# Attention and an ELU feed-forward block on one core: in the first chunk, three float32r terms for the first product of nine tiles, plain float32 for every second product

## The chip, the core and the metric

The kernel runs on one core of a Trainium2 chip. The metric is the device time of one execution in microseconds (us), the median of several runs. TensorE (PE in the profile) multiplies matrices, VectorE (DVE) and ScalarE (ACT) do elementwise work, GpSimd (POOL) a little of it, and SyncE (SP) issues the DMAs. Each engine takes its instructions strictly in the order in which the program lists them.

## The reference

```python
scores = q @ k.transpose(0, 1, 3, 2) / sqrt(D)      # 8 batches, 8 heads, 576 positions, D = 64
# heads 0-3: the last 32 positions; heads 4-7: every fourth of the last 128
attn = softmax(where(mask, scores, -1e9))
x = (attn @ v).transpose(0, 2, 1, 3).reshape(4608, 512)
h = x @ w_in                                        # w_in 512 x 2048
g = where(h > 0, h, exp(minimum(h, 0)) - 1)         # ELU
out = g @ w_out                                     # w_out 2048 x 512
```

The weights reach the kernel in float64's 64 bits (as int64), and it makes float32 of them on the chip.

## The kernel before

The 4608 rows of `x` are done in nine chunks `c` of 512, and the 2048 hidden columns in sixteen tiles `f` of 128. For each tile, `gemm1(c, f)` computes the first product into a PSUM bank (`h_ps`, two of them in turn), `elu` makes the hidden tile of it on ACT and DVE, and `gemm2`, two tiles later (`LAG`), adds that tile times its rows of `w_out` to four banks `o_ps`, which hold the chunk's output. Attention for batch `c + 1` is threaded between the tiles: score matmuls and output matmuls (`a_ps`) on PE, the softmax and the transposes on DVE and ACT.

A product comes in two forms. In plain float32 it is 4 matmuls of 512 columns, which the profile counts as 8 instructions. In three float32r terms each operand is split into a high part (a copy on ACT that rounds to float32r) and a low part (a subtraction on DVE), and the product is high times high, high times low and low times high: 12 matmuls. `split_x(c)` splits the chunk's `x` into `xh` and `xl`, `split_w` the weights into `wh` and `wl`, and a hidden tile that goes into a three-term second product is split into `gh` and `gl`, with another form of the ELU (L300 to L305). Chunks 1 to 8 use three terms throughout.

The weights come in sixteen pairs `k` of two halves, in the order in which they are needed: pair 0 holds `w_in` of tiles 0 and 1, pair `k` up to 14 `w_in` of tile `k + 1` and `w_out` of tile `k - 1` (pair 1: tiles 2 and 0), pair 15 `w_out` of tiles 14 and 15. A pair is loaded into a slot `r0` to `r7` (pair 8 into `r0` again), `magnitude` (ACT, L100) and `convert` (four DVE instructions of 1024 elements, L108 to L113) make float32 of it in a tile `a`, and only then is the slot free. Chunk 0 converts pairs 2 to 15 while it computes.

In chunk 0, tiles 0 to 11 are plain float32 in both products and tiles 12 to 15 (`F0 = 12`) three-term in both. The splits of pairs 11 to 15, whole pairs, are issued at tiles 9 to 13; `split_x(0)` is issued at tile 8, and pairs 0 to 10 are split in chunk 1. A scheduler sets the order of instructions from an estimate of its own. `issue_after(i)` only puts what the block traces on the engine of `i` behind `i`: before, `split_x(0)` stands behind a DVE instruction, so that its DVE half is held and its ACT half is free to go as early as the scheduler likes.

Of the kernel before, what the change touches and what calls it, by code (L numbers as in the profile page):

```python
# [10 lines left out]
F32 = mybir.dt.float32  # L11
F32R = mybir.dt.float32r
# [4 lines left out]
ALU = mybir.AluOpType  # L17
# [4 lines left out]
DM, DFF = H * D, 2048  # L22
NT = B * S
P = 128
# [8 lines left out]
NF = DFF // P  # L33
NC = DM // P
AHEAD = 4
NR = NF // 2
NE = 4
LAG = 2
F0 = 12
K0 = F0 - 1  # L40
NEG = -1.0e9

TINY = float(np.array([0x38000000], np.uint32).view(np.float32)[0])
# [3 lines left out]
def body(ctx: ExitStack, tc: tile.TileContext, q, k, v, masks, w_in, w_out, out):  # L47
    nc = tc.nc
    const = ctx.enter_context(tc.tile_pool(name="const", bufs=1))
    wst = ctx.enter_context(tc.tile_pool(name="wst", bufs=1))  # L50
# [13 lines left out]

    early = [wst.tile([P, 4 * DM], F32, name=f"r{NR - NE + i}") for i in range(NE)]
    for z in pt:
        nc.gpsimd.memset(z, 0.0)

    raw, full2, full = [None] * NF, [None] * NF, [None] * 2 * NF

    need = sorted(range(2 * NF), key=lambda i: i // 2 + (i % 2) * (LAG + 0.5))

    wh, wl = [None] * 2 * NF, [None] * 2 * NF
# [5 lines left out]
    def mm(*args, **kw):  # L79
        inorder(nc.tensor.matmul(*args, **kw))  # L80

    def load_w(k, behind=None):

        raw[k] = wst.tile([P, 2, DM], I64, name=f"r{k % NR}")
        if behind is not None:
            nc.gpsimd.tensor_copy(out=raw[k].bitcast(F32)[:QB, :, 0:1], in_=behind[:, 0:2].unsqueeze(2))
        for t in range(2):
            i = need[2 * k + t]
            nc.sync.dma_start(out=raw[k][:, t, :], in_=(w_in, w_out)[i % 2][i // 2])
# [6 lines left out]
    def magnitude(k):  # L96
        pair = full2[k] = wst.tile([P, 2, DM], F32, name=f"a{k}")
        for t in range(2):
            full[need[2 * k + t]] = pair[:, t, :]
        return nc.scalar.activation(out=pair.rearrange("p t c -> p (t c)"), in_=halves(k)[1].bitcast(F32), func=AF.Abs)  # L100
# [11 lines left out]

        return keep(nc.vector.scalar_tensor_tensor(out=au, in0=lo, scalar=29, in1=au, op0=ALU.logical_shift_right, op1=ALU.bitwise_or))  # L113

    def split_w(k):

        if k >= K0:
            both = wst.tile([P, 2, 2, DM], F32R, name=f"r{k - K0}")
            h, l = both[:, 0, :, :], both[:, 1, :, :]
        else:  # L120
            l = wst.tile([P, 2, DM], F32R, name=f"a{k - 1}")
            slot = NF - K0 + k // 2
            if slot < NR:
                if k % 2 == 0:
                    split_w.room = wst.tile([P, 2, 2, DM], F32R, name=f"r{slot}")
                h = split_w.room[:, k % 2, :, :]
            else:
                h = wst.tile([P, 2, DM], F32R, name=f"a{K0 + k - 2 * (NR - NF + K0)}")
        nc.scalar.copy(out=h, in_=full2[k])
        nc.vector.tensor_tensor(out=l, in0=full2[k], in1=h.bitcast(F32), op=ALU.subtract)  # L130
        for t in range(2):
            wh[need[2 * k + t]], wl[need[2 * k + t]] = h[:, t, :], l[:, t, :]

    x32 = {}
    last_step = [None] * NPAIR
# [9 lines left out]
    def load_pair(b, hp):  # L145
        i = b * NPAIR + hp
        qt, kt, vt = room(b, hp)
        nc.sync.dma_start(out=qt, in_=q[i])
        nc.sync.dma_start(out=kt, in_=k[i])
        nc.sync.dma_start(out=vt, in_=v[i])  # L150
        return qt, kt, vt
# [113 lines left out]
    hidden, below = [], []  # L265

    def split_x(c):
        for hp in range(NC):
            xh[hp] = xp.tile([P, TC], F32R, name=f"xh{hp}")
            xl[hp] = xp.tile([P, TC], F32R, name=f"xl{hp}")  # L270
            t0 = c * TC
            while t0 < (c + 1) * TC:
                b, o = divmod(t0, S)
                n = min(S - o, (c + 1) * TC - t0)
                u = slice(t0 - c * TC, t0 - c * TC + n)
                src = x32[b][:, hp, o:o + n]
                nc.scalar.copy(out=xh[hp][:, u], in_=src)
                nc.vector.tensor_tensor(out=xl[hp][:, u], in0=src, in1=xh[hp][:, u].bitcast(F32), op=ALU.subtract)
                t0 += n

    def gemm1(c, f):
        h_ps = ps_h.tile([P, TC], F32, name="h_ps")
        i = 2 * f
        if c == 0 and f < F0:
            terms = [(full[i], x32[0][:, n, :TC], n) for n in range(NC)]
        else:
            terms = [(wh[i], x[n], n) for n in range(NC) for x in (xh, xl)] + [(wl[i], xh[n], n) for n in range(NC)]
        for t, (w, x, n) in enumerate(terms):
            mm(h_ps, w[:, n * P:(n + 1) * P], x, start=t == 0, stop=t == len(terms) - 1)
        return h_ps  # L290

    def elu(h_ps, first):
        e = fp.tile([P, TC], F32, name="e", bufs=3)
        nc.scalar.activation(out=e, in_=h_ps, func=AF.Exp)  # L294
        if first:
            below.append(nc.scalar.activation(out=e, in_=e, func=AF.Relu, scale=-1.0, bias=1.0).ins)
            g = fp.tile([P, TC], F32, name="gh", bufs=3)
            hidden.append(nc.vector.scalar_tensor_tensor(out=g, in0=h_ps, scalar=0.0, in1=e, op0=ALU.max, op1=ALU.subtract).ins)  # L298
            return g, None
        nc.vector.tensor_scalar(out=e, in0=e, scalar1=1.0, scalar2=-1.0, op0=ALU.min, op1=ALU.add)  # L300
        hidden.append(nc.vector.scalar_tensor_tensor(out=e, in0=h_ps, scalar=0.0, in1=e, op0=ALU.max, op1=ALU.add).ins)  # L301
        gh = fp.tile([P, TC], F32R, name="gh", bufs=3)
        gl = fp.tile([P, TC], F32R, name="gl", bufs=2)
        nc.scalar.copy(out=gh, in_=e)  # L304
        nc.vector.tensor_tensor(out=gl, in0=e, in1=gh.bitcast(F32), op=ALU.subtract)  # L305
        return gh, gl
# [15 lines left out]
    def batch_attention(b):  # L322

        x32[b] = xp.tile([P, NPAIR, S], F32, name="x32", bufs=2)

        old = None
        for hp in range(NPAIR):
            it = attention(b, hp, loaded.pop((b, hp)))
            next(it)
            nxt = b * NPAIR + hp + 1  # L330
            if nxt < B * NPAIR:
                loaded[divmod(nxt, NPAIR)] = load_pair(*divmod(nxt, NPAIR))
            yield
            if old is not None:
                next(old)
                yield
            old = it
        next(old)
        yield
# [5 lines left out]
    for what in "m0 qk0 qk1 qk2 qk3 v0 v1 w0 v2 v3".split():  # L345
        i = int(what[-1])
# [11 lines left out]
    for what in "S0 S1 M0 M1 A0 S2 S3 P0 M2 T0 P1 M3 T1 O0 P2 T2 O1 P3 B0 T3 O2 O3 A1 C0 D1".split():  # L358
        i = int(what[1])
# [11 lines left out]
    loaded[1, 0] = load_pair(1, 0)  # L371
    for j in range(NR - NE, NR + 2):
        load_w(j)
    split = 0
    pend = []
    o_of = {}

    def flush(n):
        while len(pend) > n:
            c, f, g = pend.pop(0)  # L380
            if f == 0:
                o_of[c] = [ps_o.tile([P, DM], F32, name="o_ps") for _ in range(TC // P)]
            gemm2(o_of[c], g, f)
            if f == NF - 1:
                store(c, o_of.pop(c))

    for c in range(NCH):
        if c > 0:
            split_x(c)
        att = batch_attention(c + 1) if c + 1 < B else iter(())  # L390
        emitted = 0
        for f in range(NF):
            while c == 0 and ready < min(NF, f + AHEAD):
                with tc.issue_after(below[-1] if below else last_copy.ins):
                    magnitude(ready)
                with tc.issue_after(last_conversion.ins):
                    last_conversion = convert(ready)
                if ready + NR < NF:
                    load_w(ready + NR)
                ready += 1  # L400
            if c == 0 and f == F0 - 4:
                with tc.issue_after(hidden[-1]):
                    split_x(0)
            if c == 0 and K0 <= f + 2 < NF:
                with tc.issue_after(hidden[-1]):
                    split_w(f + 2)
            while c == 1 and split < min(K0, f + 2):

                with tc.issue_after(hidden[NF - 4 if split < 2 else NF - 1]):
                    split_w(split)  # L410
                split += 1
            pend.append((c, f, elu(gemm1(c, f), c == 0 and f < F0)))
            while emitted < (f + 1) * STEPS // (NF - 1):
                emitted += 1
                if c == 0 and emitted <= 2:
                    with tc.issue_after(last_step[NPAIR - 1]):
                        next(att, None)
                else:
                    next(att, None)
            flush(LAG)  # L420
    flush(0)
# [59 lines left out]
```

## Time and profile before

| | |
|---|---|
| median of 3 runs | 919.42 us (919.11 to 920.49) |
| profiled execution, its own time | 918.69 us |
| its span in the trace | 916.9 us |
| PE busy | 896.3 us, 98% of the span |
| DVE, ACT, POOL busy | 530.7, 393.8, 42.2 us |

The span runs from the first to the last instruction; 1.8 us of the execution's time lie around it. Times in rows below count from the span's start. A matmul's duration in the trace overlaps that of the next, so the cost of one is read from start to start.

### The profile page before, as it was taken

What the parts mean: (1) busy time and instruction counts of PE and PEld (TensorE: products, weight loads), DVE (VectorE), ACT (ScalarE), POOL (GpSimd) and SP (SyncE); (2) the same over time, 40 slices, a digit from 0 to 9 for tenths busy, and PEclk for the clock granted to TensorE, in tenths of its full rate; (3) what the DMA queues carried; (4) which work ended last, traced back from release to release, by engine and by line L of the source; (5) the groups of instructions that cost most, each with busy time, mean ns of one, the idle gap of its engine ahead of it and who ended that gap; (6) DMA issues with size and microseconds to landing.
All of it is one profiled execution on the core that took longest, in us unless ns stands there. A gap on an engine that the chain in (4) does not pass through costs nothing.

```text
span 916.9 us, 15986 instructions
## 1 busy us (share of the span) xinstructions
PE 896.3 (98%) x6536; PEld 694.4 (76%) x6536; DVE 530.7 (58%) x924; ACT 393.8 (43%) x1189; POOL 42.2 (5%) x34
## 2 busy tenths in 40 slices
PE   6799989999999999999999999999999999999998
PEld 4444458888878887888888887888788888888886
DVE  6699998775565555555475545655655533343332
ACT  4754594543354344444543445433443432233222
POOL 1000000110000000000000001000000000000000
PEclk9899999999999999999999999999999999999999
DMA  9964011211131112112211112111300010001001
GB/s 348 385 234 137 17 45 51 80 33 45 35 100 44 45 35 86 32 44 63 67 52 44 45 34 86 43 44 36 100 19 18 1 47 1 0 1 47 1 1 46
DMA packets 23801, 59.39 MB, mean 65 GB/s; under 512 B 2640, under 2 KB 2736, under 8 KB 23728
## 3 DMA queue, kind: packets, MB, share of 16 engines
q1 hardware_dynamic: 23728, 58.37, 19.2%
q8 instruction: 51, 0.84, 0.4%
q14 instruction: 22, 0.18, 0.1%
HBM read 48.92 MB, written 9.44 MB: 64 GB/s over the span
## 4 chain that ended last, share of the span: by engine, by line
PE 86%; DVE 6%; ACT 5%; DMA 2%; issue 1%; SPq 0%; ACTq 0%; DVEq 0%
PE h_ps L80 40%; PE o_ps L80 40%; PE a_ps L80 5%; ACT sm L252 3%; ACT pt L233 1%; DMA r<-w_in 1%; DVE sm L248 1%; DVE nmx L249 1%; DVE pt L258 1%; DVE a L113 1%; DMA kt<-k 1%; DVE e L301 0%; DVE r L130 0%; DVE a L111 0%; DVE gh L298 0%
## 5 line engine op out<-in xcount | busy, mean ns | idle before, releaser
L80 PE MATMUL o_ps<-a,gh 128*128 128x512 f32 x576 | 207.3, 429 | 0.0
L80 PE MATMUL o_ps<-r,gh 128*128 128x512 f32 x576 | 195.3, 398 | 0.4
L294 ACT ACTIVATE e<-h_ps 128x512 f32<-128x512 f32 x144 | 85.5, 594 | 234.7 <-PE h_ps L80 234.5
L80 PE MATMUL h_ps<-xh,r 128*128 128x512 f32 x512 | 182.6, 391 | 2.3 <-DVE e L301 2.3
L304 ACT CAST gh<-e 128x512 fp32r<-128x512 f32 x132 | 82.0, 621 | 195.6 <-DVE e L301 195.6
L300 DVE TENSOR_SCALAR e<-e 128x512 f32<-128x512 f32 x132 | 63.5, 481 | 163.5 <-ACT e L294 162.5
L80 PE MATMUL h_ps<-xh,a 128*128 128x512 f32 x480 | 147.7, 389 | 0.0
L80 PE MATMUL o_ps<-r,gl 128*128 128x512 f32 x368 | 143.5, 390 | 0.0
L80 PE MATMUL h_ps<-xl,r 128*128 128x512 f32 x368 | 143.2, 389 | 0.0
L80 PEld LDWEIGHTS o_ps<-a,gh 128*128 128x128 f32 x576 | 106.4, 188 | 39.4 <-issue 19.6
L305 DVE TENSOR_TENSOR gl<-e,gh 128x512 fp32r<-128x512 f32 x132 | 91.3, 691 | 76.1 <-PE o_ps L80 59.7
L80 PEld LDWEIGHTS o_ps<-r,gh 128*128 128x128 f32 x576 | 106.6, 188 | 27.0 <-ACT o L319 2.5
L252 ACT ACTIVATE sm<-sm,nmx 96x64 f32<-96x64 f32 x336 | 112.0, 336 | 33.5 <-DVE nmx L250 33.0
L80 PEld LDWEIGHTS h_ps<-xh,r 128*128 128x128 f32 x512 | 96.1, 188 | 23.6 <-ACT x L171 3.1
L80 PEld LDWEIGHTS h_ps<-xh,a 128*128 128x128 f32 x480 | 90.1, 188 | 18.7
L258 DVE STREAM_TRANSPOSE pt<-sm 32x384 f32<-32x384 f32 x168 | 95.5, 568 | 12.7 <-POOL sm L181 10.8
L301 DVE SCALAR_TENSOR_TENSOR e<-h_ps,e 128x512 f32<-128x512 f32 x132 | 91.1, 690 | 4.0
L80 PEld LDWEIGHTS o_ps<-r,gl 128*128 128x128 f32 x368 | 69.1, 188 | 15.2
L80 PEld LDWEIGHTS h_ps<-xl,r 128*128 128x128 f32 x368 | 69.1, 188 | 14.8 <-issue 0.5
L181 POOL TENSOR_TENSOR sm<-sm,sums 96x768 f32<-96x768 f32 x24 | 39.1, 1630 | 657.2 <-ACT e L294 321.1
L252 ACT ACTIVATION_READ_ACCUMULATOR sm<-sm,nmx 96x1 f32 x336 | 63.1, 188 | 0.0
L80 PE MATMUL o_ps<-a,gl 128*128 128x512 f32 x160 | 62.5, 391 | 0.0
(89 smaller groups left out, 699.4 us busy)
## 6 DMA issues: line engine op xcount, KB each, us to landing
vt<-v SPq DMA_DIRECT2D x30, 384.0 KB, 3.1
kt<-k SPq DMA_DIRECT2D x30, 304.0 KB, 4.1
qt<-q SPq DMA_DIRECT2D x30, 288.0 KB, 3.2
r<-w_in SPq DMA_DIRECT2D x16, 512.0 KB, 7.1
r<-w_out SPq DMA_DIRECT2D x16, 512.0 KB, 7.1
out<-o SPq DMA_DIRECT2D x32, 256.0 KB, 3.3
out<-xl SPq DMA_DIRECT2D x4, 256.0 KB, 2.1
r<-v SPq DMA_DIRECT2D x2, 384.0 KB, 8.4
```

The source lines that it names most:

```text
L80: inorder(nc.tensor.matmul(*args, **kw))
L113: return keep(nc.vector.scalar_tensor_tensor(out=au, in0=lo, scalar=29, in1=au, op0=ALU.logical_shift_right, op1=ALU.bitwise_or))
L181: return keep(eng.tensor_tensor(out=sm, in0=sm, in1=sums.unsqueeze(2).broadcast_to([QB, 2 * NU, 2 * G]), op=ALU.mult))
L233: inorder(nc.scalar.copy(out=to[ks, :, :, cs], in_=t4[rs, :, :, cs]))
L248: nc.vector.tensor_tensor(out=sm[:, h * NU:(h + 1) * NU, :].rearrange("p n j -> p (n j)"), in0=s_ps[h], in1=mask_sb[:, int(dil), :], op=AL ...
L252: nc.scalar.activation(out=sm[:, u, :], in_=sm[:, u, :], func=AF.Exp, bias=nmx[:, u:u + 1], scale=0.125, accum_out=sums[:, u:u + 1])
L258: nc.vector.transpose(out=tr[ks, :, cs], in_=sm[cs, :, rs])
L294: nc.scalar.activation(out=e, in_=h_ps, func=AF.Exp)
L300: nc.vector.tensor_scalar(out=e, in0=e, scalar1=1.0, scalar2=-1.0, op0=ALU.min, op1=ALU.add)
L301: hidden.append(nc.vector.scalar_tensor_tensor(out=e, in0=h_ps, scalar=0.0, in1=e, op0=ALU.max, op1=ALU.add).ins)
L304: nc.scalar.copy(out=gh, in_=e)
L305: nc.vector.tensor_tensor(out=gl, in0=e, in1=gh.bitcast(F32), op=ALU.subtract)
```

## The change

`F0` and `K0` go, and `F1 = 7` comes. In chunk 0 the first product is plain for tiles 0 to 6 and three-term for tiles 7 to 15, and the second is plain for all sixteen; `elu` therefore takes the plain form throughout chunk 0. Only the `w_in` half of pairs 6 to 14 is split in chunk 0, at two tiles ahead of its use; chunk 1 splits what is left, the other halves by themselves. `split_x(0)` is issued at tile 4 in place of 8, with its DVE half behind a DVE instruction and its ACT half behind an ACT instruction. A new function, `space`, hands out room for the split halves: first the eight slots `r0` to `r7`, four halves each, in turn.

```diff
+F1 = 7
-F0 = 12
-K0 = F0 - 1
...
+    spaces = [[f"r{i}", 4] for i in range(NR)] + [["a-1", 2]]
+    taken = {}
+
+    def space(n):
+
+        s = next(s for s in spaces if s[1] >= n)
+        if s[0] not in taken:
+            taken[s[0]] = wst.tile([P, s[1], DM], F32R, name=s[0]), s[1]
+        room, all_of = taken[s[0]]
+        o = all_of - s[1]
+        s[1] -= n
+        return room[:, o:o + n, :]
+
+    def split_w(k, t0, t1):
+
+        h, l = space(t1 - t0), space(t1 - t0)
+        w = full2[k][:, t0:t1, :]
+        nc.scalar.copy(out=h, in_=w)
+        nc.vector.tensor_tensor(out=l, in0=w, in1=h.bitcast(F32), op=ALU.subtract)
...
-        if c == 0 and f < F0:
+        if c == 0 and f < F1:
             terms = [(full[i], x32[0][:, n, :TC], n) for n in range(NC)]
...
-            if c == 0 and f == F0 - 4:
+            if c == 0 and f == F1 - 3:
+                with tc.issue_after(hidden[-1]), tc.issue_after(below[-1]):
+                    split_x(0)
+            if c == 0 and F1 <= f + 2 < NF:
+                j, t = divmod(need.index(2 * (f + 2)), 2)
                 with tc.issue_after(hidden[-1]):
-                    split_x(0)
-            if c == 0 and K0 <= f + 2 < NF:
-                with tc.issue_after(hidden[-1]):
-                    split_w(f + 2)
-            while c == 1 and split < min(K0, f + 2):
-
-                with tc.issue_after(hidden[NF - 4 if split < 2 else NF - 1]):
-                    split_w(split)
+                    split_w(j, t, t + 1)
+            while c == 1 and split < min(NF, f + 2):
+                left = [t for t in range(2) if wh[need[2 * split + t]] is None]
+
+                with tc.issue_after(hidden[-4 if split < 2 else -1]):
+                    split_w(split, left[0], left[-1] + 1)
                 split += 1
-            pend.append((c, f, elu(gemm1(c, f), c == 0 and f < F0)))
+            pend.append((c, f, elu(gemm1(c, f), c == 0)))
```

Three places where the order of instructions moves matter below. Line numbers in rows of the changed kernel are its own.

The first is ACT in the start-up, where attention for batch 0 is finished (`pt`: transposed probabilities; `x32`: its result; `d`, `c`, `b`, `a`: PSUM banks). Before:

```order
L174 COPY x32_106<-d_349 128x9x4x8 x2
L277 CAST xh0_926<-x32_106 128x512
L233 COPY pt1_76<-c_368 64x6x32
L233 COPY pt1_76<-c_368 32x6x32 x2
L233 COPY pt1_76<-c_368 64x6x32 x2
L233 COPY pt1_76<-c_368 32x6x32 x2
L233 COPY pt1_76<-c_368 64x6x32
L174 COPY x32_106<-b_389 128x9x4x8 x2
L277 CAST xh1_930<-x32_106 128x512
L233 COPY pt0_75<-a_412 64x6x32
```

and of the change, the same stretch:

```order
L179 COPY x32_106<-d_349 128x9x4x8 x2
L238 COPY pt1_76<-c_368 64x6x32
L238 COPY pt1_76<-c_368 32x6x32 x2
L238 COPY pt1_76<-c_368 64x6x32 x2
L238 COPY pt1_76<-c_368 32x6x32 x2
L238 COPY pt1_76<-c_368 64x6x32
L179 COPY x32_106<-b_389 128x9x4x8 x2
L238 COPY pt0_75<-a_412 64x6x32
```

The casts to `xh` have left the start-up; all four now stand behind the magnitude of pair 7.

The second is ACT around tile 7 of the change (`e_840` is the ELU of tile 6, `e_871` that of tile 7, `a6` to `a11` are pairs 6 to 11, `r0_794` is the room for the first split halves):

```order
L299 ACTIVATE e_840<-h_ps_835 128x512
L301 ACTIVATE e_840<-e_840 128x512
L99 ACTIVATE a10_849<-r2_513 128x1024
L132 CAST r0_794<-a6_654 128x512
L132 CAST r0_794<-a7_749 128x512
L299 ACTIVATE e_871<-h_ps_858 128x512
L132 CAST r1_855<-a8_788 128x512
L132 CAST r1_855<-a9_827 128x512
L301 ACTIVATE e_871<-e_871 128x512
```

Before, nothing stood between the magnitude of pair 10 and tile 7's first instruction: the casts are new here. The first of them has a wait for DVE, the second has none of its own.

The third is DVE at the same point of the change; `a8_788<-r0_501` are the last two conversion steps of pair 8, which lies in slot `r0`, and `gh_843` is the ELU of tile 6:

```order
L110 SCALAR_TENSOR_TENSOR a8_788<-r0_501,a8_788 128x1024
L263 STREAM_TRANSPOSE pt0_75<-sm_673 32x12x32 x6
L112 SCALAR_TENSOR_TENSOR a8_788<-r0_501,a8_788 128x1024
L107 TENSOR_SCALAR a9_827<-a9_827 128x1024
L303 SCALAR_TENSOR_TENSOR gh_843<-h_ps_835,e_840 128x512
L109 TENSOR_SCALAR a9_827<-a9_827 128x1024
L133 TENSOR_TENSOR r0_794<-a6_654,r0_794 128x512
L133 TENSOR_TENSOR r0_794<-a7_749,r0_794 128x512
```

The low halves for tiles 7 and 8 come three instructions behind the conversion of pair 8. Ahead of it DVE does what it did before, a few small softmax steps shifted, and with it the four subtractions of `split_x(0)`: they now stand around the end of pair 5's conversion, and before stood inside that of pair 10.

## Rows read from the trace of the kernel before

**Rows 1.** The page: busy time, share of the span and instructions of each engine.

```profile
PE 896.3 (98%) x6536; PEld 694.4 (76%) x6536; DVE 530.7 (58%) x924; ACT 393.8 (43%) x1189; POOL 42.2 (5%) x34
```

**Rows 2.** Timeline of ACT in the start-up: start, length, line, what, idle time before.

```profile
24.66 0.62 ACT L277 CAST xh<-x 128x512 fp32r<-128x512 f32 x1
25.19 2.58 ACT L233 COPY pt<-c 64x192 f32<-64x192 f32 x8
...
34.16 0.70 ACT L171 COPY x<-b 128x288 f32<-128x288 f32 x2 [2.46 <-PE b L80]
```

**Rows 3.** Timeline of PE at the end of the start-up.

```profile
27.82 1.20 PE L80 MATMUL d<-pt,r 128*64 128x96 f32 x22 [0.93 <-ACT pt L233]
...
31.94 2.18 PE L80 MATMUL b<-pt,r 128*64 128x96 f32 x22 [1.19 <-DVE pt L231]
34.91 8.77 PE L80 MATMUL h_ps<-x,a 128*128 128x512 f32 x16 [0.79 <-ACT x L171]
```

**Rows 4.** Stretches: from:to, length, PE busy (instructions), granted clock, DMA share, GB/s.

```profile
11.45:13.68 2.23, 0.00 (x1) 1.00 1.00 396
...
14.34:17.75 3.41, 3.30 (x96) 0.50 1.04 395
...
133.11:135.41 2.30, 0.00 (x1) 1.00 0.00 0
```

**Rows 5.** Timeline of PE: plain products, alternating products, three-term products.

```profile
74.51 3.60 PE L80 MATMUL h_ps<-x,a 128*128 128x512 f32 x8
...
81.38 3.60 PE L80 MATMUL h_ps<-x,a 128*128 128x512 f32 x8
...
122.01 3.59 PE L80 MATMUL o_ps<-a,gh 128*128 128x512 f32 x8
...
128.27 1.21 PE L80 MATMUL a_ps<-pt,vt 128*64 128x96 f32 x24
...
142.38 0.39 PE L80 MATMUL h_ps<-xh,r 128*128 128x512 f32 x1
...
147.82 0.39 PE L80 MATMUL h_ps<-xh,r 128*128 128x512 f32 x1
```

**Rows 6.** Timeline of DVE: tile 0's ELU, pair 8's last step, low parts.

```profile
41.57 0.69 DVE L298 SCALAR_TENSOR_TENSOR gh<-h_ps,e 128x512 f32<-128x512 f32 x1 [1.05 <-ACT e L296]
...
81.76 1.23 DVE L113 SCALAR_TENSOR_TENSOR a<-r,a 128x1024 uint32<-128x1024 uint32 x1
...
89.15 1.28 DVE L278 TENSOR_TENSOR xl<-x,xh 128x512 fp32r<-128x512 f32 x2
90.36 1.22 DVE L111 SCALAR_TENSOR_TENSOR a<-r,a 128x1024 uint32<-128x1024 uint32 x1
...
116.54 1.22 DVE L130 TENSOR_TENSOR r<-a,r 128x1024 fp32r<-128x1024 f32 x1
```

**Rows 7.** Timelines of DVE, ACT and PE up to tile 14 of chunk 0.

```profile
124.80 0.16 DVE L250 TENSOR_SCALAR nmx<-nmx 96x12 f32<-96x12 f32 x1
125.26 0.35 ACT L252 ACTIVATE sm<-sm,nmx 96x64 f32<-96x64 f32 x1
129.39 0.17 DVE L179 TENSOR_SCALAR sums<-sums 96x12 f32<-96x12 f32 x1 [1.99 <-ACT sm L252]
...
130.73 0.42 DVE L300 TENSOR_SCALAR e<-e 128x512 f32<-128x512 f32 x1
131.07 3.47 DVE L258 STREAM_TRANSPOSE pt<-sm 32x384 f32<-32x384 f32 x6
134.57 0.69 DVE L301 SCALAR_TENSOR_TENSOR e<-h_ps,e 128x512 f32<-128x512 f32 x1
135.41 0.47 PE L80 MATMUL h_ps<-xh,r 128*128 128x512 f32 x1 [2.30 <-DVE e L301]
```

**Rows 8.** Two stretches: from:to, length, PE, PEld, DVE, ACT, POOL busy, clock, DMA.

```profile
45.00:128.00 83.00, 83.00 (x456) 40.10 (x454) 81.59 (x115) 48.83 (x134) 0.00 (x0) 1.00 0.35 116
135.00:160.00 25.00, 24.59 (x193) 19.95 (x194) 22.26 (x36) 11.96 (x24) 0.00 (x0) 1.00 0.13 40
```

More of the change, by code (lines that the diff above doesn't have):

```diff
@@ L113, in convert @@
         return keep(nc.vector.scalar_tensor_tensor(out=au, in0=lo, scalar=29, in1=au, op0=ALU.logical_shift_right, op1=ALU.bitwise_or))
[L115 to L132, printed above, removed]
+    spaces = [[f"r{i}", 4] for i in range(NR)] + [["a-1", 2]]
[13 more added lines that the diff above has]
+        nc.vector.tensor_tensor(out=l, in0=w, in1=h.bitcast(F32), op=ALU.subtract)
+        for t in range(t0, t1):
+            wh[need[2 * k + t]], wl[need[2 * k + t]] = h[:, t - t0, :], l[:, t - t0, :]
+        if all(wh[need[2 * k + t]] is not None for t in range(2)):
+            spaces.append([f"a{k}", 2])
     x32 = {}
@@ L300, in elu @@
         nc.vector.tensor_scalar(out=e, in0=e, scalar1=1.0, scalar2=-1.0, op0=ALU.min, op1=ALU.add)
-        hidden.append(nc.vector.scalar_tensor_tensor(out=e, in0=h_ps, scalar=0.0, in1=e, op0=ALU.max, op1=ALU.add).ins)
+        nc.vector.scalar_tensor_tensor(out=e, in0=h_ps, scalar=0.0, in1=e, op0=ALU.max, op1=ALU.add)
         gh = fp.tile([P, TC], F32R, name="gh", bufs=3)
```

## The prediction

> **What bounds the kernel now.** I read the page first: PE is busy 98% of the span, so a change pays or costs where it alters PE's own work or makes PE wait [rows 1]. The stretches show where PE waits at all: from 45 to 128 us it runs without a gap at full clock [rows 8], at 133.11 it stands still for 2.30 us [rows 4]. Its other idle time up to there lies in the start-up, before 34.91 us. From chunk 1 on PE does the same instructions in both kernels, so the whole question is what happens up to about 160 us. There DVE is the engine to watch: it is busy for 81.59 of the 83 us from 45 to 128 [rows 8], and PE's one wait, at tile 14, ends with a DVE instruction [rows 7].
>
> The timelines give prices. Two plain products take 81.38 - 74.51 = 6.87 us, 3.43 each; two three-term products take 147.82 - 142.38 = 5.44 us, 2.72 each; a plain one and a three-term one in turn take 128.27 - 122.01 = 6.25 us, 0.10 more than the mean of the two kinds [rows 5].
>
> **The change, part by part.** All terms are differences to the profiled execution, whose own time is 918.69 us, 0.73 us below the median of 919.42.
>
> *Start-up.* ACT sets the pace there: its copies of `pt` follow one another, and PE and DVE wait for them. The cast at 24.66 us holds the next copy to 25.19, 0.53 us [rows 2]; a second, four microseconds later, does the same. The third stands ahead of ACT's wait of 2.46 us for PE [rows 2], and the fourth ahead of its wait for tile 0; they cost nothing. Without the two, DVE's copy, PE's last attention product and its first big one at 34.91 us all come 1.05 us earlier, and so does DVE's conversion queue: **-1.05**. The least is 0, if something that I don't see ended last; the most is in the rival on the start-up clock.
>
> *The new wait at tile 7.* Tile 7's first product now needs the high part of its weights, a cast on ACT. It writes into slot `r0`, which still holds pair 8 as loaded, so it must come after pair 8's conversion. That its first cast waits for DVE and the second, of a pair converted later, has no wait of its own fits this: a wait for pair 6 alone would not cover pair 7. Pair 8's conversion ends at 81.76 + 1.23 = 82.99 us now [rows 6]. DVE is saturated up to there, so it comes 1.05 us earlier by the start, and later by the four subtractions of `split_x(0)` that now stand ahead of it: two take 90.36 - 89.15 = 1.21 us, four 2.4 [rows 6]. That makes 84.35, with the cast (0.62 us, as in rows 2) 85.0. PE would begin tile 7 at 81.38 - 1.05 = 80.33 us [rows 5]. It waits **4.7 us**. The low part follows four DVE instructions later, at 84.26 + 3 x 0.60 + 0.69 = 86.75 us, about when PE has done the eight matmuls that use the high part (8 x 0.227 us from 85.05): no second wait. Bounds: 0, if the cast waits for pair 6 alone, which is converted two pairs earlier; 5.8, if the start-up gains nothing for DVE.
>
> Behind that cast on ACT's queue stand the second cast and tile 7's ELU, which can't begin before tile 7 is done anyway; behind tile 7's first ELU instruction stand the casts into `r1`, which wait for pair 9 (three DVE instructions and two subtractions after pair 8), before its second. The ELU of tile 7 is needed two products later. I set this at 0.
>
> *The clock.* An idle stretch of 2.23 us of PE was followed by a fall of the granted clock to 0.50, for 3.41 us in which PE was busy for 3.30; the 2.30 us at tile 14 was followed by none [rows 4]. The first big products ran at 0.50 too, after a start-up full of gaps: the first two took 8.77 us in place of 6.87 + 0.17 (the overlap), 1.7 to 1.8 lost [rows 3]. An idle stretch twice as long, in a dense run of products, I take to be followed by such a fall, at the same price: **1.7 us**. Bounds: 0 (as after 2.30 us) and 3.4, two such stretches.
> [...]
>
> *PE's work up to tile 14.* Tiles 7 to 11 take a three-term product for a plain one, in alternation with plain second products: (6.87 - 6.25) x 5 = **-3.1** [rows 5]. Tiles 12 and 13 had one before. PE would come to tile 14 at 133.11 - 1.05 + 4.7 - 3.1 = 133.7 us, or 135.4 with the clock.
>
> *The old wait at tile 14.* PE needs the PSUM bank of tile 12, which DVE frees. That chain goes: maxima ready on DVE at 124.96 us, twelve exponentials on ACT from 125.26 (ACT was busy with a cast until then), sums at 129.39, normalisation to 130.73, the ELU's L300, six transposes from 131.07 to 134.57, L301 to 135.26, PE at 135.41 [rows 7]. In the change the maxima come at 124.96 - 1.05 + 0.25 = 124.15: both kernels have the four `xl` before that point, but eight half pairs at 0.60 us (half of 1.21) replace four whole ones at 1.14 (1.22 less the overlap that the `xl` rows show) [rows 6]. The casts of chunk 1's weights no longer crowd ACT there, so the exponentials begin at 124.2; 4.13 us of them, 1.34 to the end of the normalisation, 3.50 of transposes, 0.69 of ELU and 0.15 to PE make 134.0 us. L300 is gone. So tile 14 begins at 134.0 us without the clock's fall, PE just waiting, and at 135.4 with it, where PE comes last and the old wait is gone. Against 135.41 that is **-1.4 or 0.0**. Note what this does: the chain on DVE gives back nothing of the 3.1 us that PE saves, and hides up to that much of the wait at tile 7.
>
> *The end of chunk 0.* Four second products, tiles 12 to 15, become plain: 4 x (3.43 - 2.72) = 2.84 us, and the four three-term products behind them pay 0.10 each for the alternation; a plain product behind an attention step loses less than a three-term one by some 0.2. **+3.0**. Nothing covers it: PE is busy for 24.59 of 25 us there [rows 8]. Bounds 2.6 and 3.3.
>
> *Chunk 1.* DVE splits seven whole pairs and nine halves, 7 x 1.14 + 9 x 0.60 = 13.4 us, for eleven whole ones, 12.5; but it loses L300 and the subtraction to `gl` on four tiles (about 1 us each). Its share of 22.26 of 25 us from 135 to 160 us [rows 8] falls, and PE did not wait there: 0. If that cover were gone, PE would wait for an ELU at some tiles of chunk 1, about 1 us each.
>
> **Sum.** 0.0 + 3.0 = +3.0 with the fall of the clock: 918.69 + 3.0 = 921.7 for an execution like the profiled one, and by the median 919.42 + 3.0 = **922.4 us**. About 0.2% (1.84 us) is what a measurement of this kernel can tell from no change.
>
> **Rivals.**
> - *No fall of the clock, or no wait at tile 7* (the cast waits for pair 6 alone, so that this part of the change is harmless). PE then comes to tile 14 at 133.7 or 129.0 us, and in both cases DVE's chain lets it go on at 134.0. -1.4 + 3.0 = +1.6: 921.0 us, not measurably slower. For it: the 2.30 us without a fall. Against it: the 2.23 us with one, and the slot's second use. It decides as soon as the clock's loss is under 0.3 us.
> - *The start-up runs at full clock.* Its gaps shrink by 1.05 us, and if the clock stays up, PE's attention product at 31.94 us takes 1.20 in place of 2.18 us, as the same one did at 27.82, and the first products lose no 1.7 [rows 3]. The first 0.98 us move DVE as well, of the 1.7 only the 1.05 for which DVE waits for tile 0's ELU [rows 6]. All comes about 2.0 us earlier: 922.4 - 2.0 = 920.4 us, not slower, and 919.0 together with the first rival. Against it: between 29.02 and 31.94 us PE does next to nothing [rows 3], and the change takes away only half a microsecond of that. It decides if the clock is up when the product at 31.94 begins.
> - *ACT's queue passes the wait on.* The casts into `r1`, `r2` and `r3` stand ahead of ELU instructions and each waits for a conversion two pairs on; or the clock falls for two stretches. One more wait or stretch of 1.7 us: 924.1 us. Against it: from tile 8 on PE is late against DVE, so conversions have gained on it.
>
> **How the numbers follow.** The forecast 0.50, the first rival 0.23, the second 0.15, the third 0.12. From 919.3 to 924.6 us leaves out about 2 in 10: the far ends of the second and third rival and errors of about 0.7 us on the others. The forecast's own range is 921.3 to 923.6. Faster by over 0.2% (below 917.6) needs the second rival and more: 0.05. Within 0.2%: the first rival, nearly all of the second, a little of the forecast's lower edge less a little of the first's upper: 0.33. Slower: 0.62.
>
> **What would show it.** In the profile after: the `xh` casts gone from the start-up and the first big product at 33.8 to 33.9 us; an idle stretch of PE of 4 to 5.5 us in tile 7's first product, put down to ACT's cast or to DVE's last conversion step; a granted clock of 0.50 for some 3 to 4 us behind it; tile 14 beginning between 134 and 136 us with little or no wait; no wait of PE after it. The prediction is wrong if PE doesn't wait at tile 7, if the clock is at 0.50 anywhere else, or if PE waits in chunk 1.

## The result, and the profile after

The changed kernel takes 922.0 us in the median (919.85 to 924.42) against 920.11 us (919.09 to 921.44) for the kernel before, measured beside it: a ratio of 1.0022 with a 95% interval of [1.0014, 1.0031], so 1.3 to 2.9 us slower. The profiled execution of after took 923.32 us (span 921.5), 1.3 us above its median; where that shows below, it is said.

The page of after: busy time of the engines, and the group of tile 7's kind of product (line engine operation, count | busy, mean ns | idle time ahead of it and what ended most of it).

```profile
PE 899.4 (98%) x6540; PEld 697.9 (76%) x6540; DVE 525.5 (57%) x925; ACT 395.1 (43%) x1198; POOL 41.6 (5%) x34
...
L79 PE MATMUL h_ps<-xh,r 128*128 128x512 f32 x936 | 315.3, 396 | 4.6 <-ACT r L132 4.6
```

PE is busy 3.1 us longer than in [rows 1], and a wait of 4.6 us for ACT's cast (L132) is new. The timelines of ACT, PE and DVE at the end of the start-up, with start, length, line, what, and idle time before:

```profile
25.17 2.67 ACT L238 COPY pt<-c 64x192 f32<-64x192 f32 x8
31.39 2.18 PE L79 MATMUL b<-pt,r 128*64 128x96 f32 x22 [1.19 <-DVE pt L236]
33.60 0.70 ACT L176 COPY x<-b 128x288 f32<-128x288 f32 x2 [3.12 <-PE b L79]
34.36 10.08 PE L79 MATMUL h_ps<-x,a 128*128 128x512 f32 x16 [0.79 <-ACT x L176]
42.38 0.69 DVE L303 SCALAR_TENSOR_TENSOR gh<-h_ps,e 128x512 f32<-128x512 f32 x1 [2.41 <-ACT e L301]
```

No cast stands between ACT's copies any more. The first big product begins 0.55 us earlier than in [rows 3], but the first two take 10.08 us in place of 8.77: the clock stayed at 0.50 longer in this execution (30.08 to 40.32 us, before 31.41 to 38.23). So they end 0.76 us later than before, and tile 0's ELU on DVE, for which DVE's conversions wait, begins at 42.38, 0.81 us later than in [rows 6]. Around tile 7, on PE, DVE and ACT:

```profile
78.70 3.60 PE L79 MATMUL o_ps<-a,gh 128*128 128x512 f32 x8
84.94 1.22 DVE L112 SCALAR_TENSOR_TENSOR a<-r,a 128x1024 uint32<-128x1024 uint32 x1
86.20 1.14 ACT L132 CAST r<-a 128x512 fp32r<-128x512 f32 x2 [4.99 <-DVE a L112]
86.87 0.80 PE L79 MATMUL h_ps<-xh,r 128*128 128x512 f32 x1 [4.57 <-ACT r L132]
91.97 0.97 PE L79 MATMUL a_ps<-kt,qt 64*32 64x64 f32 x72
```

DVE ends the last step of pair 8's conversion at 86.16, ACT's cast into `r0` follows at 86.20, PE at 86.87. ACT kept to its listed order: the casts into `r1` begin at 92.57, behind tile 7's first ELU instruction (92.07, after 4.73 us of waiting for PE), though pair 9's conversion ended at 91.56. The same place as stretches (from:to, length, PE busy, granted clock, DMA share, GB/s):

```profile
82.30:86.87 4.57, 0.00 (x0) 0.76 0.01 4
86.87:91.27 4.40, 4.40 (x10) 0.50 0.00 0
```

The clock falls while PE still stands idle, at 84.7 us, and stays at 0.50 until 91.5, for 4.6 us of dense work. At tile 14 and behind it:

```profile
126.24 0.16 DVE L255 TENSOR_SCALAR nmx<-nmx 96x12 f32<-96x12 f32 x1
133.73 3.70 PE L79 MATMUL o_ps<-a,gh 128*128 128x512 f32 x8
135.52 0.69 DVE L303 SCALAR_TENSOR_TENSOR gh<-h_ps,e 128x512 f32<-128x512 f32 x1
136.86 0.79 PE L79 MATMUL h_ps<-xh,r 128*128 128x512 f32 x1
141.26 3.70 PE L79 MATMUL o_ps<-a,gh 128*128 128x512 f32 x8
147.56 3.59 PE L79 MATMUL o_ps<-a,gh 128*128 128x512 f32 x8
153.73 3.59 PE L79 MATMUL o_ps<-a,gh 128*128 128x512 f32 x8
```

Tile 14's product (136.86) has no wait: DVE's chain, which ended the old one of 2.30 us [rows 7], is done at 136.21. Behind it a second product and the first product that follows take 6.30 and 6.17 us, where such a pair took 5.44 [rows 5].

### The profile page after: what moved, and what is told of

The parts are those of the page before. It is cut to its first block, busy times and chain, and to the rows that moved or that the text cites. A ratio compares the mean times of both kernels' runs of the same rounds, so it can differ in the third digit from the quotient of the medians.

```text
span 921.5 us, 16002 instructions
## 1 busy us (share of the span) xinstructions
PE 899.4 (98%) x6540; PEld 697.9 (76%) x6540; DVE 525.5 (57%) x925; ACT 395.1 (43%) x1198; POOL 41.6 (5%) x34
## 4 chain that ended last, share of the span: by engine, by line
PE 86%; DVE 6%; ACT 5%; DMA 1%; issue 1%; SPq 0%; ACTq 0%; DVEq 0%
PE o_ps L79 41%; PE h_ps L79 39%; PE a_ps L79 5%; ACT sm L257 2%; DMA r<-w_in 1%; ACT pt L238 1%; DVE a L110 1%; DVE a L112 1%; DVE nmx L254 1%; DVE sm L253 1%; DVE pt L263 1%; DMA kt<-k 1%; DVE a L107 0%; DVE a L109 0%; ACT e L299 0%
## 5 line engine op out<-in xcount | busy, mean ns | idle before, releaser
L79 PE MATMUL o_ps<-a,gh 128*128 128x512 f32 x960 | 320.7, 423 | 0.0
L79 PE MATMUL h_ps<-xh,r 128*128 128x512 f32 x936 | 315.3, 396 | 4.6 <-ACT r L132 4.6
L79 PEld LDWEIGHTS o_ps<-a,gh 128*128 128x128 f32 x960 | 176.6, 188 | 60.5 <-issue 24.4
L79 PEld LDWEIGHTS h_ps<-xh,r 128*128 128x128 f32 x936 | 176.8, 189 | 44.8 <-ACT r L132 5.4
L79 PE MATMUL h_ps<-xl,r 128*128 128x512 f32 x484 | 189.4, 391 | 0.0
L79 PE MATMUL o_ps<-a,gl 128*128 128x512 f32 x416 | 162.2, 390 | 0.0
L79 PEld LDWEIGHTS h_ps<-xl,r 128*128 128x128 f32 x484 | 91.5, 189 | 21.4 <-issue 2.4
L79 PEld LDWEIGHTS o_ps<-a,gl 128*128 128x128 f32 x416 | 78.1, 188 | 17.3
L79 PE MATMUL o_ps<-r,gh 128*128 128x512 f32 x160 | 53.2, 397 | 0.4
L79 PE MATMUL h_ps<-xh,a 128*128 128x512 f32 x128 | 42.0, 389 | 0.0
L79 PE MATMUL o_ps<-r,gl 128*128 128x512 f32 x96 | 37.5, 390 | 0.0
```

## The experiments

Times are medians, each compared with the kernel before on the same chip; "the changed kernel" is 922.0 us, ratio 1.0022. Diffs are against the changed kernel unless it says otherwise.

**The slot: room that holds nothing.**

```diff
-    spaces = [[f"r{i}", 4] for i in range(NR)] + [["a-1", 2]]
+    spaces = [["a-1", 2]] + [[f"r{i}", 4] for i in range(NR)]
```

> The changed kernel, but the first two split halves (tile 7's weights) go into a room that has held nothing, in place of slot r0; tile 8's halves are the first in r0. Theory A (the wait of 4.6 us at tile 7 is the cast waiting for pair 8 to leave r0): no wait of PE at tile 7, and no clock of 0.50 behind it. PE then comes to tile 14 some 6.8 us earlier (4.6 of wait and 2.2 of clock), near 130.5 us of the span, but the chain on DVE, which ended at 136.2 us in the changed kernel, still ends there: so a wait of 5 to 6 us for DVE at tile 14, and a gain of only about 1.0 us on the changed kernel, near 921.0 us; if the clock falls behind that longer wait, the gain is lost again (922 to 923 us). Theory B (the cast waits for something else, such as pair 6's own conversion or ACT's queue): the wait at tile 7 stays at 4 to 5 us and the time is that of the changed kernel.

920.59 us, ratio 1.0004 [0.9996, 1.0013]. PE's timeline has no wait at tile 7, but one at tile 14:

```profile
132.69 0.50 PE L79 MATMUL h_ps<-xh,r 128*128 128x512 f32 x1 [3.26 <-DVE gh L303]
```

Its stretches there:

```profile
129.43:132.69 3.26, 0.00 (x1) 1.00 0.00 0
133.00:136.35 3.35, 3.35 (x10) 0.56 0.02 5
```

Theory A holds for the wait: it was the slot. Its picture of the rest was only half right. The chain on DVE did not stay at 136.2 us; it ended at 132.64, so the wait was 3.3 and not 5 to 6 us. But the clock fell behind it, and wait and clock together gave back most of what the slot had cost: 1.4 us are left against the changed kernel, where A had none for the case that the clock falls (922 to 923 us).

**F1 = 9.**

```diff
-F1 = 7
+F1 = 9
```

> The changed kernel with F1 = 9: tiles 7 and 8 stay plain in the first product, so that the first cast into r0 is wanted two tiles later. Theory A (the wait at tile 7 is one for slot r0, and what lies ahead of tile 14 is bound by DVE's chain): PE does 1.2 us more of its own work, yet waits nowhere before tile 14, and the clock stays up; DVE's chain ends about 1.2 us earlier (two half subtractions fewer), tile 14 begins near 135 us with a wait of 3 to 4 us; 1.5 to 2.5 us faster than the changed kernel, 919.5 to 920.5 us. Theory B (the three-term products of tiles 7 and 8 are worth what they save, and the wait would only move): 1.2 us slower than the changed kernel or the same.

921.76 us, ratio 1.0016 [1.0007, 1.0025]: a miss for A, which wanted 1.5 to 2.5 us. B's number, the same time with the wait moved, fits. No wait at tile 7 or 9 in the trace (of the fastest of the eleven executions, 920.02 us), but on DVE and PE at tile 14:

```profile
128.74 2.95 DVE L133 TENSOR_TENSOR r<-a,r 128x512 fp32r<-128x512 f32 x3
131.61 3.47 DVE L263 STREAM_TRANSPOSE pt<-sm 32x384 f32<-32x384 f32 x6
135.18 1.91 PE L79 MATMUL a_ps<-pt,vt 128*64 128x96 f32 x24 [3.04 <-issue]
```

The scheduler, which orders by its own estimate, put three splits (one for tile 15, two for chunk 1) ahead of the last transposes; in the changed kernel they stand behind them. The attention product that reads the transposes waits until they end (131.61 + 3.47 = 135.08), 3.04 us, and the clock is at 0.50 from 135.5 to 138.9 us. The edit changed two things, so it can't be read as meant.

**Filling the idle time.** A plain product goes into tile 7's bank first:

```diff
+        if c == 0 and f == F1:
+            for n in range(NC):
+                mm(h_ps, full[i][:, n * P:(n + 1) * P], x32[0][:, n, :TC], start=n == 0, stop=n == NC - 1)
```

> The changed kernel with a plain product put ahead of tile 7's three-term product, into the same bank, which the three-term product then overwrites: 3.4 us of work more for PE, done in the time in which it waits for the cast. Theory A (the fall of the clock follows PE's idle stretch): the idle stretch shrinks from 4.6 to about 1.2 us, the three-term product begins at the same time as before (near 86.9 us), and the clock doesn't fall; PE gains the 2.2 us behind it, of which DVE's chain at tile 14 lets about 1.0 through: 0.5 to 1.2 us faster than the changed kernel with more work. Theory B (the clock falls there for another reason, or falls after 1.2 us as well): the clock is at 0.50 for 3 to 4 us all the same, and the time is that of the changed kernel.

923.59 us, ratio 1.0042 [1.0029, 1.0056], by the median 1.6 us above the changed kernel, where A wanted 0.5 to 1.2 us below it. Its stretches:

```profile
83.62:84.74 1.12, 0.00 (x1) 1.00 0.00 0
84.74:88.00 3.26, 3.26 (x43) 1.00 0.00 0
135.92:138.52 2.60, 0.00 (x1) 1.00 0.00 0
138.95:142.70 3.75, 3.75 (x24) 0.54 0.37 109
```

At tile 7 A is right: the idle time is 1.12 us and the clock stays at 1.00. At tile 14 DVE had the three splits ahead of the transposes again (132.08 to 135), PE waited 2.60 us, and there the clock fell. The total says nothing of tile 7; the last group of runs repeats this with the order set.

**The start-up alone**, on the kernel before:

```diff
-                with tc.issue_after(hidden[-1]):
+                with tc.issue_after(hidden[-1]), tc.issue_after(below[-1]):
                     split_x(0)
```

> The kernel before, with one edit: the casts of x's high parts also stand behind an ACT instruction of the running tile, so that they leave the start-up; products, splits and slots are those of before. Theory A (ACT's copies set the pace of the start-up, and two of the four casts stand in that chain): the first big product and all DVE work behind it come 0.5 to 1.05 us earlier, tile 14 still begins when DVE's chain ends, and the kernel is 0.5 to 1.05 us faster than before. Theory B (another chain or the low clock of the start-up ends last, so that the casts were free): the first big product begins at 34.7 to 35.0 us, and the time is that of before within 0.2 us.

918.7 us, ratio 0.9986 [0.9975, 0.9996]: A, with 1.3 us (0.4 to 2.3). PE's timeline:

```profile
34.09 9.13 PE L80 MATMUL h_ps<-x,a 128*128 128x512 f32 x16 [0.79 <-ACT x L171]
...
134.97 0.47 PE L80 MATMUL h_ps<-xh,r 128*128 128x512 f32 x1 [2.33 <-DVE e L301]
```

The product begins 0.82 us earlier than in [rows 3], the first two end 0.46 us earlier, and the old wait at tile 14 is as long as it was.

**Three-term second products for tiles 12 to 15 again.**

```diff
+F2 = 12
...
-        nc.vector.scalar_tensor_tensor(out=e, in0=h_ps, scalar=0.0, in1=e, op0=ALU.max, op1=ALU.add)
+        hidden.append(nc.vector.scalar_tensor_tensor(out=e, in0=h_ps, scalar=0.0, in1=e, op0=ALU.max, op1=ALU.add).ins)
...
-                    split_w(j, t, t + 1)
+                    if f < F2:
+                        split_w(j, t, t + 1)
+                    else:
+                        split_w(j, 0, 2)
+            if c == 0 and f == NF - 2:
+                with tc.issue_after(hidden[-1]):
+                    split_w(NF - 1, 0, 2)
...
-                with tc.issue_after(hidden[-4 if split < 2 else -1]):
-                    split_w(split, left[0], left[-1] + 1)
+                if left:
+                    with tc.issue_after(hidden[NF - 4 if split < 2 else NF - 1]):
+                        split_w(split, left[0], left[-1] + 1)
...
-            pend.append((c, f, elu(gemm1(c, f), c == 0)))
+            pend.append((c, f, elu(gemm1(c, f), c == 0 and f < F2)))
```

> The changed kernel with the second product of tiles 12 to 15 of chunk 0 in three terms again, as before the change: their hidden tiles take the longer form of the ELU, and pairs 13 to 15 are split whole in chunk 0. Tile 7's slot, its wait and the first products stay as changed. Theory A (those four products in plain float32 cost 2.8 to 3.3 us that nothing covers): PE waits 4 to 5 us at tile 7 as in the changed kernel, and the time is 2.5 to 3.3 us below it, about 919 us. Theory B (DVE, which then has more splits and longer ELUs there, takes the gain back in waits at the end of chunk 0 or the start of chunk 1): 0 to 1.5 us below it, with waits of PE for DVE between 137 and 170 us.

919.05 us, ratio 0.9993 [0.9982, 1.0003]: A. PE's timeline:

```profile
86.20 0.73 PE L80 MATMUL h_ps<-xh,r 128*128 128x512 f32 x1 [4.56 <-ACT r L133]
...
90.73 0.97 PE L80 MATMUL a_ps<-kt,qt 64*32 64x64 f32 x72
...
132.49 3.70 PE L80 MATMUL o_ps<-a,gh 128*128 128x512 f32 x8
```

From tile 11's second product (132.49, and 133.73 in the changed kernel) to the end of the span (917.4 and 921.5) it is 784.9 us against 787.8: 2.86 us for the four products, with no new wait. The wait at tile 7 is as before, and the product behind it takes 90.73 - 86.20 = 4.53 us here against 5.10 in the changed kernel: the same fall of the clock has two prices in two executions.

**Both edits**: the free room and the three-term second products.

> The kernel of the run before, and also tile 7's split halves in the unused room in place of slot r0: three-term first products from tile 7, no wait for a slot, three-term second products for tiles 12 to 15. Theory A (the slot's wait and the plain second products are all that the change lost): no wait at tile 7, and the 3.0 us of the end are back: about 3 us below the run with the free room alone, 917 to 918 us, faster than the kernel before by 2 to 3 us. If a wait of over 2.5 us for DVE stands at tile 14 or 15, as the 3.3 us in that run did, the clock falls behind it and 1.7 us of this are lost: 919 to 920 us. Theory B (DVE's work ahead of tile 14 bounds chunk 0, whatever PE does): within 0.5 us of the kernel before.

919.43 us, ratio 0.9992 [0.9982, 1.0002]: A with its second clause; but B's number, within 0.5 us of the kernel before (919.77 beside it), fits as well. PE's timeline at tile 14:

```profile
135.45 1.40 PE L80 MATMUL a_ps<-pt,vt 128*64 128x96 f32 x24 [3.76 <-issue]
```

Two splits stood ahead of the transposes (131.88 to 135.35), PE waited 3.76 us, and the clock was at 0.50 from 136.3 to 139.7 us. Against the free room alone it is 1.2 us in the medians and 3.2 between the two profiled executions (the one here, 917.23 us, is the fastest of twelve); how much of the 3.0 arrives, these two runs leave open. B is ruled out only by the runs below with DVE's order set.

**DVE's order at tile 14**, on the kernel before with its start-up mended. The generator of the last attention step pauses ahead of its transposes, and goes on behind tile 12's ELU:

```diff
         tr = transposed()
+        if (b, hp) == (1, NPAIR - 1):
+            held.append(True)
+            yield
...
+            if c == 0 and f == 12:
+                with tc.issue_after(hidden[-1]):
+                    next(held[0])
```

> The kernel before with the start-up casts moved, as in the run with that alone, and one more edit: the six transposes of the last attention step of chunk 0 are put behind tile 12's ELU instruction on DVE, in place of ahead of it, so that the bank for tile 14 comes free 3.5 us earlier. Theory A (PE's old wait at tile 14 is the transposes' length): the wait of 2.3 us is gone, tile 14 begins at 132 to 132.6 us, and the time is 2.0 to 2.4 us below the run with the start-up alone, 916.3 to 916.7 us; the attention product behind it, which needs the transposes, waits at most 0.7 us. Theory B (the wait only moves to that product): PE waits some 2 us there, and the time is that of the run with the start-up alone, 918.7 us.

916.51 us, ratio 0.9959 [0.9947, 0.9971]: A, 2.2 us below the start-up alone. DVE and PE there:

```profile
130.57 0.69 DVE L304 SCALAR_TENSOR_TENSOR e<-h_ps,e 128x512 f32<-128x512 f32 x1
131.17 3.48 DVE L261 STREAM_TRANSPOSE pt<-sm 32x384 f32<-32x384 f32 x6
131.90 0.79 PE L80 MATMUL h_ps<-xh,r 128*128 128x512 f32 x1
137.70 0.50 PE L80 MATMUL o_ps<-r,gl 128*128 128x512 f32 x1 [0.67 <-DVE gl L308]
```

Compare [rows 7]: the ELU step of 0.69 us now stands ahead of the 3.47 us of transposes, and the 2.30 us of waiting have shrunk to 0.67 at another place.

**F1 = 12**: no three-term first product before tile 12, as before the change; the rest as changed.

```diff
-F1 = 7
+F1 = 12
```

> The changed kernel with F1 = 12: the first product plain for tiles 0 to 11 as before the change, the second plain throughout, the start-up as changed. No split half is wanted before tile 12, and PE saves nothing on tiles 7 to 11. Theory A (the end's plain second products cost 3.0 us, the start-up gives 0.5 to 1.3 us, tile 14 still begins when DVE's chain ends): no wait at tile 7, a wait of up to 2.5 us at tile 14, and 1.7 to 2.5 us above the kernel before, 921.7 to 922.5 us, the same as the changed kernel: its three-term first products are worth nothing. Theory B (the three-term first products do pay, and the wait and clock at tile 7 only take a part back): 1.5 us or more above the changed kernel, 923.5 us or more.

921.07 us, ratio 1.0012 [1.0003, 1.0022]: nearer to A, 0.6 us below its range. PE's wait at tile 14:

```profile
134.97 0.50 PE L79 MATMUL h_ps<-xh,r 128*128 128x512 f32 x1 [1.44 <-DVE gh L303]
```

So the three-term first products of tiles 7 to 11, on which PE saves some 3 us of work, made the changed kernel no faster than this one without them: by the medians 0.9 us slower, with intervals that overlap.

**The changed kernel with DVE's order set, and two edits of it.** The control has the pause of the transposes shown above, and the splits of chunk 1's first two pairs later:

```diff
-                with tc.issue_after(hidden[-4 if split < 2 else -1]):
+                with tc.issue_after(hidden[-2 if split < 2 else -1]):
```

> The changed kernel with DVE's order at tile 14 set: tile 12's ELU ahead of the six transposes of the last attention step, and the splits of chunk 1's first two pairs behind tile 14's ELU. It is the control for the next two runs. Theory A (in the changed kernel PE comes to tile 14 about 1 us after DVE, so that nothing there waits for DVE): the wait of 4.6 us at tile 7 stays, no wait at tile 14, and the time is that of the changed kernel within 0.7 us, 921.3 to 922.7 us. Theory B (DVE's order at tile 14 is what costs in the changed kernel, too): 2 us or more faster.

Then the control with the filling product:

> The run before with the plain product put ahead of tile 7's three-term product, which overwrites it, as in the first run with that filling product; now DVE's order at tile 14 can't be another one. Theory A (the clock falls because PE stands idle for 4.6 us, and that costs 1.7 to 2.2 us): PE waits about 1.2 us, the clock stays up at tile 7, the three-term product begins no later than without the filling, tile 14 begins about 2 us earlier and nothing waits for DVE behind it: 1.5 to 2.2 us faster than the control, with 3.4 us more work of PE. Theory B (the clock's fall costs nothing that shows, since DVE is the bound): the same as the control within 0.5 us.

and the control with the free room:

> The control with tile 7's split halves in the unused room in place of slot r0. Theory A (the slot costs the wait and the clock behind it, and in the first run with the free room DVE's order at tile 14 took most of that back): no wait at tile 7, at most 1 us of waits at tile 14 and the attention product behind it, no clock of 0.50 after the start-up; 4.5 to 5.5 us faster than the control, 916.5 to 917.5 us. Theory B (the total of DVE's work ahead of tile 14 is the bound, and order doesn't matter): not below 919.5 us.

The control: 921.79 us, ratio 1.0020 [1.0011, 1.0029], as A said. PE's timeline, the wait at tile 7 and the first instruction behind the product:

```profile
85.80 0.50 PE L79 MATMUL h_ps<-xh,r 128*128 128x512 f32 x1 [4.56 <-ACT r L132]
...
90.33 0.97 PE L79 MATMUL a_ps<-kt,qt 64*32 64x64 f32 x72
```

With the filling, 921.3 us, ratio 1.0013 [1.0004, 1.0021]:

```profile
86.51 0.50 PE L79 MATMUL h_ps<-xh,r 128*128 128x512 f32 x1 [1.13 <-ACT r L132]
...
89.47 0.97 PE L79 MATMUL a_ps<-kt,qt 64*32 64x64 f32 x72
...
138.03 1.21 PE L79 MATMUL a_ps<-pt,vt 128*64 128x96 f32 x24 [0.34 <-issue]
```

Behind 1.13 us of idle time the product takes 2.96 us at full clock, behind 4.56 us it takes 4.53: 1.57 us is what the clock cost, and 0.34 come back as a wait. From the start of tile 7's three-term product to the end of the span (919.6 us, 920.0 for the control) that is 833.1 against 834.2 us, 1.1 us less; the filling's 3.4 us of work lie ahead of it, in what was idle time. The medians differ by only 0.5 us, less than their intervals can tell: A's mechanism is in the traces, but its total of 1.5 to 2.2 us was missed, and 0.5 is what B had.

With the free room, 916.0 us, ratio 0.9957 [0.9944, 0.9969]: A, 5.8 us below the control, 0.3 us more than its range; B (not below 919.5 us) is out. PE at tile 7 and behind tile 14:

```profile
80.52 0.80 PE L79 MATMUL h_ps<-xh,a-1_794 128*128 128x512 f32 x1
...
132.66 1.21 PE L79 MATMUL a_ps<-pt,vt 128*64 128x96 f32 x24 [0.38 <-issue]
```

This is the price of the slot where next to nothing hides it: no wait at tile 7, and 0.38 us behind tile 14.

**All of it**: the free room, the order, and the three-term second products for tiles 12 to 15.

> The free room and DVE's order as in the run before, and three-term second products for tiles 12 to 15 as in the kernel before the change; pair 14 is split one tile later. Theory A (the terms add up): the 3.0 us of the plain second products come off as well, with a wait of up to 2 us for the transposes behind tile 14 and no fall of the clock: 913.5 to 915.5 us, faster than both kernels and than the kernel before with its start-up and order mended (916.5 us). Theory B (the longer ELUs and whole splits put DVE behind again, with a wait of over 2.5 us and the clock falling behind it): 917 us or more.

915.22 us, ratio 0.9954 [0.9940, 0.9967], by the median the fastest kernel of this study: 4.2 us below the kernel before by the ratio, and 6.8 below the changed one by the medians. It lies within A's range, but only 0.8 us below the run before, not 3.0, and with five executions each their intervals overlap. PE shows where the rest went:

```profile
132.60 1.21 PE L80 MATMUL a_ps<-pt,vt 128*64 128x96 f32 x24 [1.32 <-issue]
...
142.69 0.39 PE L80 MATMUL h_ps<-xh,r 128*128 128x512 f32 x1
143.02 0.50 PE L80 MATMUL h_ps<-xl,r 128*128 128x512 f32 x1
143.36 0.40 PE L80 MATMUL h_ps<-xh,r 128*128 128x512 f32 x1
...
144.70 0.50 PE L80 MATMUL h_ps<-xl,r 128*128 128x512 f32 x1 [0.18 <-DVE xl L287]
```

1.32 us go to the transposes, 0.94 us more than in the run before, and chunk 1's first product steps at 0.33 us in place of 0.23: it follows the low parts of `x` as DVE makes them, and takes 3.96 us (142.03 to 145.99). Relieved at tile 14, DVE is late again at the start of chunk 1.

## Why the prediction was right, and what was mis-sized

It forecast slower: the wait and the clock at tile 7 eat up what the start-up and the three-term products gain, and the plain second products behind tile 14 then cost 3.0 us that nothing covers. That is what happened. That 922.4 us stands so near to 922.0 is in part luck: the difference to the kernel before was put at +3.0 us and is +2.0 (1.3 to 2.9), and the kernel before gave 920.11 in place of the 919.42 us that the sum began with.

*Start-up, -1.05.* Right in mechanism. From the place of the first cast to PE's last attention product it is 7.28 us before (24.66 to 31.94, [rows 2] and [rows 3]) and 6.22 in after (25.17 to 31.39), 1.06 us less. By itself the edit gave 1.3 us (0.4 to 2.3). In the profiled execution of after ACT was 0.5 us late already at the first of these points, and the longer low clock took back the rest and more. That moved all that follows by some 1.8 us, so two of the signs missed: the first big product at 34.36 in place of 33.8 to 33.9 us, tile 14 at 136.86 in place of 134 to 136. The rival of a start-up at full clock was posed as one outcome of 15 in 100. It is no property of the kernel: with the same start-up code, the attention product that took 2.18 us in [rows 3] takes 2.18 us in after (granted clock 0.50) and 1.21 in the run with F1 = 9 (1.00), and in the profiles of the experiments on the changed kernel the first big product begins anywhere from 33.23 to 35.37 us. That may be a good part of the 4.6 us by which the changed kernel's runs differ; with one trace for each kernel it isn't shown.

*The wait at tile 7, 4.7 us.* 4.57 measured, released by the step that was named; the free room takes it away. Both its ends came some 1.9 us later than in the sum, as the start-up did. The low part was in time, as said, and the second wait of the third rival did not come: behind tile 7 PE waits nowhere in after.

*The clock, 1.7 us.* It fell, and so it did in the other two traces with this wait. That it would fall was the author's estimate: of the two idle stretches in [rows 4], 2.23 us were followed by a fall and 2.30 by none, and the trace of before has none of 4.7 us. The price was 5.10 - 2.96 = 2.14 us in the profiled execution of after, and 1.57 in two others.

*PE's saving, -3.1, and the old wait at tile 14.* The old wait is gone and PE comes last, as in the sum's branch with the clock's fall. From the end of the first two products to tile 14's start it is 91.73 us before (34.91 + 8.77 = 43.68 to 135.41) and 92.42 in after (34.36 + 10.08 = 44.44 to 136.86): +0.69, and +0.12 if the clock's fall had cost 1.57. The sum had +1.05 here (0.0 with the -1.05 of the start-up). The term that was mis-sized most, besides the clock, is the old wait, taken as its idle time of 2.30 us. A three-term product that need not wait begins ahead of the end that the profile gives the product before it (in after at 136.86, where 133.73 + 3.70 makes 137.43), so the wait had cost 0.57 us more, 2.87.

DVE's chain came later than the sum had it: maxima ready at 126.24 + 0.16 = 126.40 and not at 124.15 us, the end at 136.21 and not at 133.85 (134.0 with the 0.15 us to PE). Nearly all of this is the start-up again. Tile 0's ELU began at 42.38 in place of 41.57 - 1.05 = 40.52 us, and from there to the maxima it is 84.02 us where the sum had 83.63. It didn't count, since PE, as late as DVE, came another 0.65 us after it (and the control with DVE's order set is no faster). The step was worked out with DVE's old order. That held in after; but the runs show that an edit ahead of tile 14 can make a new one: with the free room it is 80.70 us from tile 0's ELU (41.35) to the maxima (122.05). That PE's saving would not arrive holds in this change: F1 = 12, without it, is no slower. It is no limit of DVE's total work, as the free room with the order set shows (916.0 us).

*The end of chunk 0, +3.0.* 2.86 us, by the run that undoes it; 3.15 between the traces of before and after, from tile 14's start to the end of the span.

What the parts make with these sizes: -1.3 for the start-up by itself, +0.1 to +0.7 from there to tile 14, +2.9 to +3.2 behind it, together +1.7 to +2.6; the measured +2.0 lies inside.

## What to carry to other kernels

Before a product moves onto split operands earlier, look up in whose buffer its first split lands and what must leave it: here one unused room in place of a slot was worth 5.8 us once next to nothing behind it waited. A wait of TensorE cost more here than its idle time: 2.87 us for the 2.30 at the old tile 14, and in this chunk, from 2.60 us of idle time on, a fall of the clock behind it (1.57 and 2.14 us at tile 7). So ask whether an edit that removes one only moves it to the next late engine; and where a scheduler orders an engine, look at its new order before reading a run as a test of the edit. A short step that frees a bank belongs ahead of a long one that nobody waits for yet: that was worth 2.2 us here.

## What the runs showed of the hardware

Idle stretches of PE between dense products, and the granted clock behind them, each from the trace of one execution:

| idle, us | kernel, place | clock behind it |
|---|---|---|
| 1.12 and 1.13 | filling, tile 7 | 1.00 |
| 1.32 and 1.44 | all of it; F1 = 12, tile 14 | 1.00 |
| 2.30 and 2.33 | before; start-up alone, tile 14 | 1.00 |
| 2.60 | filling, tile 14 | 0.50, 139.1 to 142.5 us |
| 3.04 | F1 = 9, tile 14 | 0.50, 135.5 to 138.9 us |
| 3.26 | free room, tile 14 | 0.50, 133.4 to 136.8 us |
| 3.76 | both edits, tile 14 | 0.50, 136.3 to 139.7 us |
| 4.56 | second products; control, tile 7 | 0.50, 86.3 to 89.7 us; 86.5 to 89.9 us |
| 4.57 | after, tile 7 | 0.50, 84.7 to 91.5 us |

In tile 7's product the matmuls follow one another at 0.43 us where the clock is at 0.50 (after), and at 0.23 where it is at 1.00 (filling). What surprised is that two idle stretches of the same length at the same place had different prices: with 4.56 us the clock fell some 0.1 to 0.7 us after PE had begun again, with 4.57 us while it still waited, and then it stayed low for 4.6 us of work in place of 3.4. The length of the idle time alone does not decide, either: in the start-up of the kernel before, 2.23 us were followed by a fall [rows 4]; what else decides, no run here shows.
